# A gate polynomial refitted: one product moved from VectorE to a square on ScalarE, in an attention and feed-forward kernel on one core

## The chip, the cores and the metric

The kernel runs on one core of one Trainium2 chip. The metric is the device time of one execution in microseconds (us). TensorE is called PE, VectorE DVE, ScalarE ACT, GpSimd POOL and SyncE SP. The names in profile rows are those of the program's tiles without their buffer numbers; L165 is line 165 of the kernel before.

## What is computed

Causal attention by blocks of 64, over 8 batches of 8 heads with 576 positions and a head size of 64, and then a feed-forward layer with a gate of its own. All data are float32.

```python
def _attn_ref(q, k, v):                       # q, k, v: (8, 8, 576, 64)
    scores = np.matmul(q, k.transpose(0, 1, 3, 2)) / np.sqrt(64)
    scores = np.where(block_i >= block_j, scores, -1e9)   # blocks of 64 positions
    attn = np.exp(scores - np.max(scores, axis=-1, keepdims=True))
    attn = attn / (np.sum(attn, axis=-1, keepdims=True) + 1e-09)
    return np.matmul(attn, v)

def _moe_ref(x, w_in, w_out):                 # x: (4608, 512), w_in: (512, 2048)
    h = x @ w_in
    sp = np.maximum(h, 0.0) + np.log1p(np.exp(-np.abs(h)))
    g = h * erf(sp)
    return g @ w_out
```

The part that matters here is g = h * erf(softplus(h)). The factor erf(softplus(h)) is a smooth step, and the kernel computes it as a polynomial in tanh.

## The kernel before

The 64 heads are worked through one after the other (the loop at L650, one turn a head). For each head, POOL's queue and SP's queue load q and k (L383 to L385), POOL splits them into a high and a low part (L388, L389), PE computes scores for row maxima (L400), DVE reduces them (L403), PE computes the transposed scores (L446, L447), ACT takes the exponential (L451), and from the fourth batch on ACT and DVE split the probabilities into two float16 parts (L462, L463). PE multiplies with v (L495) and sums rows (L518). After each pair of heads the result is normalised (L577) and stored as a high and a low float16 part in a DRAM tile x_d (L579, L580).

The feed-forward layer runs in tiles of T = 256 tokens, 18 of them, and in units of two blocks of 128 hidden columns. There are 16 blocks, taken in two groups of 8 (g = 0 and 1), so each group has 4 units and the whole kernel 18 x 8 = 144 units. A unit is made by moe_unit: 24 matmuls up (L190: high and low parts of x with high and low parts of the weights) fill a PSUM tile h of 128 x 512, the gate makes from it a high part gh and a low part gl in float16, and 12 matmuls down (L199) add their products to a PSUM tile o. A unit's down steps are queued three units behind its up steps (LAG = 3). After the last unit of a group, store scales o into DRAM: for the first group through ACT (L242), for the second through DVE, which adds the first group's part (L240).

The gate works on one h tile of 128 x 512 in the buffers r0 (three of them) and r1 (two). ACT computes the tanh (L159; in two or more calls where a tile crosses two batches) and two squares (L160, L161), DVE three products that stay in SBUF (L162, L163, L164) and the final step, which reads h from PSUM (L165). Then ACT casts to float16 (L166) and POOL takes the remainder (L167). The h tile comes free with L165. There are two h tiles while attention runs (pool ps_h) and four after it (ps_h2).

What sets the order: the program lists attention and feed-forward steps in an interleaved order (merge, with 12 or 28 feed-forward steps a head, RATE), and the tile framework's scheduler then places every instruction into its engine's queue by its dependencies and its own estimates. Each engine takes its queue strictly in order, so a row that waits holds up every row behind it. After the last head the loop at L701 runs the remaining units alone.

Of the kernel before, what the change touches and what calls it, by code (L numbers as in the profile page):

```python
# [13 lines left out]
AF = mybir.ActivationFunctionType  # L14
ALU = mybir.AluOpType
# [2 lines left out]
PSUM = bass.MemoryType.PSUM  # L18

GS = 2.0**-16  # L20
PAR = (0.4999584099340646, -0.7997936477435295, [(-0.46191564159745396, 0.41170731705509067), (0.6792666015498814, 0.003215831458770746), (1.8262741166576089,), (-0.004337242892183685,), (-2.7410929714529355,)], 0.9999991931998524)


def f32(ap):
# [8 lines left out]
def tile_attention_moe(ctx: ExitStack, tc: tile.TileContext, qk, v, w, maskrows, sels, out):  # L33
    nc = tc.nc
# [39 lines left out]
    bias = {}  # L74

    def const(val):
        if val not in bias:
            t = cpool.tile([P, 1], F32, name=f"c{len(bias)}")
            nc.gpsimd.memset(t, val)
            bias[val] = t  # L80
        return bias[val]

    p0, p1, pars, fin = PAR
    (a1, b1), (a2, b2), (c3,), (c4,), (c5,) = pars
    R8, R4, R2 = GS**0.125, GS**0.25, GS**0.5
    a2, b2, c3, c5, fin = a2 * R8, b2 * R8, c3 * R4, c5 * R2, fin * GS
    eps = const(1e-9)
    for val in (p1, b1, b2):
        const(val)

    slots = [wpool.tile([P, 4, DM], F16, name=f"w{f}") for f in range(NF + 1)]
# [58 lines left out]
    def gate(h, name, t, g):  # L150

        nu = h.shape[1]
        n = nu * T
        flat = h.rearrange("p a b -> p (a b)")
        gh, gl = (mpool.tile([P, n], F16, tag=t_, name=f"{name}_{t_}", bufs=LAG + 1) for t_ in ("gh", "gl"))
        r0, r1 = (mpool.tile([P, n], F32, tag=t_, name=f"{name}_{t_}", bufs=k) for t_, k in (("r0", 3), ("r1", 2)))
        r0s = r0.rearrange("p (a b) -> p a b", b=T)
        for b, lo, hi in spans(t * T, T):
            nc.scalar.activation(r0s[:, :, lo:hi], h[:, :, lo:hi], AF.Tanh, bias=const(p1), scale=bss[b][g][:, 0:1])  # L159
        nc.scalar.activation(r1, r0, AF.Square, bias=const(b1), scale=a1)  # L160
        nc.scalar.activation(r0, r1, AF.Square, bias=const(b2), scale=a2)  # L161
        nc.vector.scalar_tensor_tensor(out=r0, in0=r0, scalar=c3, in1=r0, op0=ALU.add, op1=ALU.mult)  # L162
        nc.vector.scalar_tensor_tensor(out=r0, in0=r1, scalar=c4, in1=r0, op0=ALU.add, op1=ALU.mult)  # L163
        nc.vector.scalar_tensor_tensor(out=r0, in0=r0, scalar=c5, in1=r0, op0=ALU.add, op1=ALU.mult)  # L164
        nc.vector.scalar_tensor_tensor(out=r0, in0=r0, scalar=fin, in1=flat, op0=ALU.add, op1=ALU.mult)  # L165
        nc.scalar.copy(gh, r0)  # L166
        nc.gpsimd.tensor_tensor(out=gl, in0=r0, in1=gh, op=ALU.subtract)  # L167
        return gh, gl

    def spans(t0, n):  # L170

        for b in range(t0 // S, (t0 + n - 1) // S + 1):
            yield b, max(0, b * S - t0), min(n, (b + 1) * S - t0)
# [4 lines left out]
    def moe_unit(xh, xl, o, t, u, u0, u1, spread):  # L178

        turns.append(u)  # L180
        nu, name = 2, f"m{t}_{u}"
        h = hpools[len(turns) % len(hpools)].tile([P, nu, T], F32, tag="h", name=f"{name}_h")
        parts = []

        def up(k, cs):
            wf = wt[u * nu + k]
            for cc in cs:
                sl = slice(cc * P, (cc + 1) * P)
                for i, (a, x) in enumerate(((0, xh), (0, xl), (1, xh))):
                    nc.tensor.matmul(h[:, k, :], lhsT=wf[:, a, sl], rhs=x[:, cc, :], start=cc == 0 and i == 0, stop=cc == NCC - 1 and i == 2)  # L190
            if k == nu - 1 and cs[-1] == NCC - 1:
                parts.extend(gate(h, name, t, group[u * nu]))

        def down(k, c, lo):
            gh, gl = parts
            wf = wt[u * nu + k]
            sl = slice(k * T + c * P, k * T + (c + 1) * P)
            for a, b_ in (((gl, 2),) if lo else ((gh, 2), (gh, 3))):
                nc.tensor.matmul(o[c], lhsT=a[:, sl], rhs=wf[:, b_, :], start=u == u0 and k == 0 and not lo and b_ == 2,  # L199
                                 stop=u == u1 - 1 and k == nu - 1 and lo)  # L200

        edge = u in (u0, u1 - 1) or not spread
        return ([lambda k=k, cs=cs: up(k, cs) for k in range(nu) for cs in ((0, 1), (2, 3))],
                [lambda a=a: down(*a) for a in sorted(((k, c, lo) for k in range(nu) for c in range(T // P) for lo in (False, True)),
                                                      key=lambda a: (a[1], a[2], a[0]) if edge else (a[2], a[0], a[1]))])
# [534 lines left out]
```

## Time and profile before

| | |
|---|---|
| median of 3 runs | 1267.88 us (1267.43 to 1275.67) |
| profiled execution | 1269.5 us, its span 1267.5 us |
| granted TensorE clock, mean | 0.969 |
| mean of one tanh (L159), square (L160, L161) | 666, 720, 720 ns |
| mean of one product (L162, L163, L164), final step (L165) | 825, 840, 787, 679 ns |
| mean of one cast (L166), remainder (L167) | 617, 1220 ns |

The means are over the whole run. The span runs from the first to the last instruction, and the two microseconds beyond it lie around the program. A row of the profile's groups names line, engine, operation, output and inputs, and how often it ran; then its busy time and the mean of one in ns, and after the last bar the idle time of the engine just before these rows with what ended it. The chain of waits is followed back from the last instruction, at each step to what released it.

### The profile page before, as it was taken

To read this page: it belongs to the slowest core of one execution; us is meant where nothing else is said; L and a number is where in the kernel's file an instruction comes from. 1 tells how busy PE (TensorE), PEld (TensorE's weight loads), DVE (VectorE), ACT (ScalarE), POOL (GpSimd) and SP (SyncE) were. 2 spreads that over 40 slices of the span, in tenths; PEclk is the share of its full clock that TensorE was granted. 3 is DMA by queue.
4 is the path that set the end of the run, shared out by engine and by line. 5 is a ranking of instruction groups with operands and counts; after the bars stand their busy time and mean duration, and the time that the engine had idled before them with its cause. 6 is when DMAs were issued, how large, how long until landed. Compare 5 with 4: busy or idle time off the path is not lost.

```text
span 1267.5 us, 23446 instructions
## 1 busy us (share of the span) xinstructions
PE 1174.1 (93%) x9018; PEld 812.4 (64%) x9018; DVE 899.5 (71%) x1601; ACT 778.0 (61%) x1555; POOL 521.3 (41%) x485
## 2 busy tenths in 40 slices
PE   5698798989999999999999999999999999999996
PEld 3465465566666666667667676766667766666563
DVE  4587698888677777887768777778777755464554
ACT  2465575667565666666666666665766765555543
POOL 6355454536443343545434453535444313212211
PEclk9777799999999999999999999999999999999999
DMA  9987568654444455354444554454444221121111
GB/s 235 221 211 191 140 186 196 168 131 114 111 120 112 120 120 126 98 141 118 100 115 117 122 124 116 116 125 118 109 126 116 58 68 58 54 83 35 59 58 50
DMA packets 95740, 151.72 MB, mean 120 GB/s; under 512 B 7738, under 2 KB 44922, under 8 KB 95630
## 3 DMA queue, kind: packets, MB, share of 16 engines
q1 hardware_dynamic: 69840, 93.34, 25.3%
q0 software_dynamic: 25120, 56.66, 22.2%
q8 instruction: 71, 1.16, 0.4%
q10 hardware_dynamic: 670, 0.23, 0.1%
q14 instruction: 39, 0.32, 0.1%
HBM read 121.66 MB, written 28.31 MB: 118 GB/s over the span
## 4 chain that ended last, share of the span: by engine, by line
PE 37%; DVE 30%; ACT 17%; DMA 8%; issue 5%; POOL 2%; ACTq 0%; DVEq 0%; SPq 0%; POOLq 0%
PE m_h L190 12%; PE o L199 11%; DVE m_r L163 6%; DVE m_r L162 5%; DVE m_r L164 5%; DVE m_r L165 4%; ACT m_r L159 4%; ACT m_r L160 4%; ACT m_r L161 4%; PE u L495 4%; DMA qk<-qk 2%; PE t L446 2%; DVE mx L403 2%; PE s L400 2%; DMA qk<-mt 2%
## 5 line engine op out<-in xcount | busy, mean ns | idle before, releaser
L190 PE MATMUL m_h<-xh,w 128*128 128x256 f16 x2304 | 477.2, 276 | 25.6 <-DVE m_r L165 18.5
L190 PEld LDWEIGHTS <-w 128*128 128x128 f16 x3456 | 328.0, 99 | 164.2 <-issue 33.7
L167 POOL TENSOR_TENSOR m_gl<-m_r,m_gh 128x512 f16<-128x512 f32 x144 | 175.6, 1220 | 423.5 <-ACT m_gh L166 365.2
L199 PE MATMUL o<-w,m_gh 128*128 128x512 f16 x1152 | 335.4, 383 | 12.2 <-DVE pt L240 8.6
L190 PE MATMUL m_h<-xl,w 128*128 128x256 f16 x1152 | 317.1, 275 | 0.3 <-DMA xl<-x_d 0.3
L162 DVE SCALAR_TENSOR_TENSOR m_r<-m_r 128x512 f32<-128x512 f32 x144 | 118.8, 825 | 189.8 <-ACT m_r L161 172.8
L403 DVE TENSOR_REDUCE mx<-s 64x1 f32<-64x288 f32 (+4 forms) x384 | 174.4, 469 | 83.8 <-PE s L400 82.6
L451 ACT ACTIVATE p<-t 128x288 f32<-128x288 f32 (+4 forms) x384 | 144.8, 384 | 99.5 <-PE t L447 89.0
L166 ACT CAST m_gh<-m_r 128x512 f16<-128x512 f32 x144 | 88.8, 617 | 188.6 <-DVE m_r L165 188.1
L199 PE MATMUL o<-w,m_gl 128*128 128x512 f16 x576 | 203.6, 383 | 0.3 <-POOL m_gl L167 0.3
L446 PE MATMUL t<-qk 69*128 69x288 f32 (+4 forms) x384 | 168.4, 439 | 11.2 <-DMA qk<-mt 8.0
L400 PE MATMUL s<-qk 68*64 68x288 f32 (+3 forms) x384 | 151.3, 425 | 27.0 <-DMA qk<-qk 21.9
L159 ACT ACTIVATE m_r<-m_h,c,bs 128x512 f32<-128x512 f32 (+3 forms) x192 | 124.3, 666 | 57.4 <-PE m_h L190 55.1
L388 POOL TENSOR_TENSOR qk<-st,qk 64x576 fp32r<-64x576 f32 x64 | 96.9, 1514 | 116.7 <-DMA qk<-qk 113.9
L199 PEld LDWEIGHTS <-m_gh 128*128 128x128 f16 x1152 | 100.5, 99 | 68.0 <-issue 17.3
L163 DVE SCALAR_TENSOR_TENSOR m_r<-m_r,m_r 128x512 f32<-128x512 f32 x144 | 121.0, 840 | 2.8
L447 PE MATMUL t<-qk 128*128 128x288 f32 (+4 forms) x384 | 120.4, 314 | 0.0
L164 DVE SCALAR_TENSOR_TENSOR m_r<-m_r 128x512 f32<-128x512 f32 x144 | 113.3, 787 | 2.4
L389 POOL TENSOR_TENSOR qk<-st,qk 64x576 fp32r<-64x576 f32 x64 | 99.3, 1552 | 35.9 <-DMA qk<-qk 28.1
L463 DVE TENSOR_TENSOR p<-p,p 128x832 f16<-128x832 f32 x80 | 84.0, 1050 | 34.8 <-ACT p L462 34.8
L161 ACT ACTIVATE m_r<-m_r,c 128x512 f32<-128x512 f32 x144 | 103.7, 720 | 2.8 <-ACT m_r L160 1.0
L160 ACT ACTIVATE m_r<-m_r,c 128x512 f32<-128x512 f32 x144 | 103.7, 720 | 1.7
(99 smaller groups left out, 1457.9 us busy)
## 6 DMA issues: line engine op xcount, KB each, us to landing
qk<-qk POOLq DMA_DIRECT2D x64, 432.0 KB, 5.0
st<-qk SPq DMA_DIRECT2D x64, 288.0 KB
qk<-qk POOLq DMA_DIRECT2D x64, 288.0 KB, 5.3
raw<-w SPq DMA_DIRECT2D x32, 512.0 KB
v<-v SPq DMA_DIRECT2D x16, 640.0 KB
x_d<-xs POOLq DMA_DIRECT2D x32, 288.0 KB, 3.9
xh<-x_d SPq DMA_DIRECT2D x36, 256.0 KB
xl<-x_d SPq DMA_DIRECT2D x36, 256.0 KB
```

The source lines that it names most:

```text
L159: nc.scalar.activation(r0s[:, :, lo:hi], h[:, :, lo:hi], AF.Tanh, bias=const(p1), scale=bss[b][g][:, 0:1])
L160: nc.scalar.activation(r1, r0, AF.Square, bias=const(b1), scale=a1)
L161: nc.scalar.activation(r0, r1, AF.Square, bias=const(b2), scale=a2)
L162: nc.vector.scalar_tensor_tensor(out=r0, in0=r0, scalar=c3, in1=r0, op0=ALU.add, op1=ALU.mult)
L163: nc.vector.scalar_tensor_tensor(out=r0, in0=r1, scalar=c4, in1=r0, op0=ALU.add, op1=ALU.mult)
L164: nc.vector.scalar_tensor_tensor(out=r0, in0=r0, scalar=c5, in1=r0, op0=ALU.add, op1=ALU.mult)
L167: nc.gpsimd.tensor_tensor(out=gl, in0=r0, in1=gh, op=ALU.subtract)
L190: nc.tensor.matmul(h[:, k, :], lhsT=wf[:, a, sl], rhs=x[:, cc, :], start=cc == 0 and i == 0, stop=cc == NCC - 1 and i == 2)
L199: nc.tensor.matmul(o[c], lhsT=a[:, sl], rhs=wf[:, b_, :], start=u == u0 and k == 0 and not lo and b_ == 2, stop=u == u1 - 1 and k == nu - ...
L400: nc.tensor.matmul(dst[:r, :w_], lhsT=qh[:K, i * P : i * P + r], rhs=kh[:K, k0 : k0 + w_], start=True, stop=True)
L403: nc.vector.tensor_reduce(out=mx[:r, col : col + 1], in_=src, axis=AX.X, op=ALU.max, negate=True)
L446: nc.tensor.matmul(s[:kk, :w_], lhsT=kh[:K, ks], rhs=qh[:K, q0 : q0 + w_], start=True, stop=False)
```

## The change

The step function is fitted anew, with another arrangement of the same kind of operations. With t the tanh, u the first square and v the second, the polynomial before was, up to constants, y = (v + c3) v, z = (u + c4) y, w = (z + c5) z, and the result (w + fin) h. Now a third square s of an affine function of v replaces y, z = (s + c4) u, and the rest stays: three squares on ACT, two products and the final step on DVE.

```diff
-PAR = (0.4999584099340646, -0.7997936477435295, [(-0.46191564159745396, 0.41170731705509067), (0.6792666015498814, 0.003215831458770746), (1.8262741166576089,), (-0.004337242892183685,), (-2.7410929714529355,)], 0.9999991931998524)
+PAR = (0.49996096731559087, -0.7971597824113146, [(-0.3568271365965769, 0.32141033078193654), (-0.6157408373309642, -4.092496034124806e-06), (4.2811914462809915, 1.199366796860444), (-1.4383868560728355,), (-2.741088145004764,)], 1.0000005263157887)
...
-    (a1, b1), (a2, b2), (c3,), (c4,), (c5,) = pars
-    R8, R4, R2 = GS**0.125, GS**0.25, GS**0.5
-    a2, b2, c3, c5, fin = a2 * R8, b2 * R8, c3 * R4, c5 * R2, fin * GS
+    (a1, b1), (a2, b2), (a3, b3), (c4,), (c5,) = pars
+    R4, R2 = GS**0.25, GS**0.5
+    a3, b3, c4, c5, fin = a3 * R4, b3 * R4, c4 * R2, c5 * R2, fin * GS
     eps = const(1e-9)
-    for val in (p1, b1, b2):
+    for val in (p1, b1, b2, b3):
         const(val)
...
         nc.scalar.activation(r1, r0, AF.Square, bias=const(b1), scale=a1)
         nc.scalar.activation(r0, r1, AF.Square, bias=const(b2), scale=a2)
-        nc.vector.scalar_tensor_tensor(out=r0, in0=r0, scalar=c3, in1=r0, op0=ALU.add, op1=ALU.mult)
-        nc.vector.scalar_tensor_tensor(out=r0, in0=r1, scalar=c4, in1=r0, op0=ALU.add, op1=ALU.mult)
+        nc.scalar.activation(r0, r0, AF.Square, bias=const(b3), scale=a3)
+        nc.vector.scalar_tensor_tensor(out=r0, in0=r0, scalar=c4, in1=r1, op0=ALU.add, op1=ALU.mult)
         nc.vector.scalar_tensor_tensor(out=r0, in0=r0, scalar=c5, in1=r0, op0=ALU.add, op1=ALU.mult)
         nc.vector.scalar_tensor_tensor(out=r0, in0=r0, scalar=fin, in1=flat, op0=ALU.add, op1=ALU.mult)
```

The line numbers stay: L162 is a product on DVE before and the third square on ACT after, L163 and L164 are the two products, L165 the final step. The constant b3 is one more tile, set by POOL at the start.

Since the scheduler goes by the operations it finds, the rows around the gate change places as well. Below is ACT's queue around the gate of one unit (tile m_5, while head 26 gives way to head 27), before. Rows of p are exponentials and casts of the attention, mt belongs to the row maxima, m_6 to the next gate.

```order
L159 ACTIVATE m_5_r_4378<-m_5_h,c_83,bs_1_113 128x2x192
L451 ACTIVATE p_1_140<-t_26_256_4399 128x320
L160 ACTIVATE m_5_r_4379<-m_5_r_4378,c_85 128x512
L462 CAST p_26_4138<-p_1_140 128x768
L161 ACTIVATE m_5_r_4378<-m_5_r_4379,c_87 128x512
L451 ACTIVATE p_0_139<-t_27_0_4422 128x288
L451 ACTIVATE p_0_139<-t_27_288_4448 128x288
L432 CAST mt_4460<-mt_4458 5x128
L433 DMA qk_126<-mt_4460 1x5x128
L159 ACTIVATE m_6_r_4473<-m_6_h,c_83,bs_1_111 128x2x64
L166 CAST m_5_gh<-m_5_r_4378 128x512
```

The same place of ACT's queue after the change.

```order
L159 ACTIVATE m_5_r_4380<-m_5_h,c_83,bs_1_115 128x2x192
L451 ACTIVATE p_1_142<-t_26_256_4401 128x320
L160 ACTIVATE m_5_r_4381<-m_5_r_4380,c_85 128x512
L462 CAST p_26_4140<-p_1_142 128x768
L161 ACTIVATE m_5_r_4380<-m_5_r_4381,c_87 128x512
L451 ACTIVATE p_0_141<-t_27_0_4424 128x288
L162 ACTIVATE m_5_r_4380<-m_5_r_4380,c_89 128x512
L451 ACTIVATE p_0_141<-t_27_288_4450 128x288
L432 CAST mt_4462<-mt_4460 5x128
L433 DMA qk_128<-mt_4462 1x5x128
L159 ACTIVATE m_6_r_4475<-m_6_h,c_83,bs_1_113 128x2x64
L166 CAST m_5_gh<-m_5_r_4380 128x512
```

One exponential that stood behind the last square now stands ahead of it. DVE's queue for the same gate, before; mx are the attention's row maxima, pt an accumulated output tile.

```order
L463 TENSOR_TENSOR p_26_4138<-p_1_140,p_26_4138 128x768
L162 SCALAR_TENSOR_TENSOR m_5_r_4378<-m_5_r_4378 128x512
L403 TENSOR_REDUCE mx_145<-s_29_4432 128x1
L163 SCALAR_TENSOR_TENSOR m_5_r_4378<-m_5_r_4379,m_5_r_4378 128x512
L403 TENSOR_REDUCE mx_145<-s_29_4432 128x1
L164 SCALAR_TENSOR_TENSOR m_5_r_4378<-m_5_r_4378 128x512
L240 SCALAR_TENSOR_TENSOR pt_0_4395<-o_1_0_3729,bs_1_111,pt_0_4395 128x512
L165 SCALAR_TENSOR_TENSOR m_5_r_4378<-m_5_r_4378,m_5_h 128x512
```

And after.

```order
L463 TENSOR_TENSOR p_26_4140<-p_1_142,p_26_4140 128x768
L403 TENSOR_REDUCE mx_147<-s_29_4434 128x1 x2
L163 SCALAR_TENSOR_TENSOR m_5_r_4380<-m_5_r_4380,m_5_r_4381 128x512
L240 SCALAR_TENSOR_TENSOR pt_0_4397<-o_1_0_3731,bs_1_113,pt_0_4397 128x512
L164 SCALAR_TENSOR_TENSOR m_5_r_4380<-m_5_r_4380 128x512
L403 TENSOR_REDUCE mx_147<-s_29_4456 128x1
L165 SCALAR_TENSOR_TENSOR m_5_r_4380<-m_5_r_4380,m_5_h 128x512
```

Two reductions left the gate for the place ahead of its first product, and one came in. In the last units, where no attention is left, ACT's queue before reads as follows.

```order
L159 ACTIVATE m_1_r_14536<-m_1_h,c_83,bs_0_124 128x512
L160 ACTIVATE m_1_r_14537<-m_1_r_14536,c_85 128x512
L161 ACTIVATE m_1_r_14536<-m_1_r_14537,c_87 128x512
L159 ACTIVATE m_2_r_14593<-m_2_h,c_83,bs_0_124 128x512
L160 ACTIVATE m_2_r_14594<-m_2_r_14593,c_85 128x512
L166 CAST m_1_gh<-m_1_r_14536 128x512
L161 ACTIVATE m_2_r_14593<-m_2_r_14594,c_87 128x512
```

After the change the same two gates stand so.

```order
L159 ACTIVATE m_1_r_14538<-m_1_h,c_83,bs_0_126 128x512
L160 ACTIVATE m_1_r_14539<-m_1_r_14538,c_85 128x512
L161 ACTIVATE m_1_r_14538<-m_1_r_14539,c_87 128x512
L162 ACTIVATE m_1_r_14538<-m_1_r_14538,c_89 128x512
L159 ACTIVATE m_2_r_14595<-m_2_h,c_83,bs_0_126 128x512
L166 CAST m_1_gh<-m_1_r_14538 128x512
L160 ACTIVATE m_2_r_14596<-m_2_r_14595,c_85 128x512
```

The next gate's first square (L160 of m_2) stood ahead of the cast of m_1 and now stands behind it.

## The prediction

> **What bounds the kernel now.** I read the page's busy times first, then three stretches, then the chain of waits of each stretch, then the instructions of each stretch. The first 150 us hold attention and weight conversion and only the start of the first gate, so they are left aside. The page, the table by stretch, and that of L165 alone for one stretch: 13 gates end in 150 to 300 us, 88 in 300 to 1000 us (rows below), and so 43 of the 144 after that.
>
> ```profile
> PE 1174.1 (93%) x9018; PEld 812.4 (64%) x9018; DVE 899.5 (71%) x1601; ACT 778.0 (61%) x1555; POOL 521.3 (41%) x485
> ...
> core 0: us, PE busy (x) PEld busy (x) DVE busy (x) ACT busy (x) POOL busy (x), PEclk, DMA share, GB/s
> 150.00:300.00 150.00, 135.98 (x1004) 91.16 (x1003) 130.95 (x244) 100.58 (x231) 72.11 (x61) 0.97 0.62 158
> 300.00:1000.00 700.00, 679.27 (x5586) 482.80 (x5585) 529.42 (x935) 459.45 (x903) 313.17 (x284) 1.00 0.48 117
> 1000.00:1267.00 267.00, 248.68 (x1779) 166.47 (x1776) 143.61 (x210) 145.83 (x243) 58.40 (x52) 0.99 0.18 58
> ...
> 150.00:300.00 150.00, 8.71 (x13) 0.97 0.62 158
> ```
>
> PE looks like the bound: 679.3 of 700 us. But a busy PE of this profile is not PE at its peak, so the chain decides. Its shares by line for the same three stretches, in order:
>
> ```profile
> by line: PE o L199 7.6%; DMA raw<-w 7.5%; DVE w L123 7.2%; DVE w L122 7.0%; DVE m_r L163 6.0%; DVE mx L403 5.9%; DVE m_r L164 5.2%; DVE w L147 5.1%; PE m_h L190 4.9%; PE us L518 4.3%; DVE m_r L162 3.8%; DVE m_r L165 3.7%; PE s L400 3.2%; PE
> ...
> by line: PE m_h L190 16.1%; PE o L199 15.3%; DVE m_r L163 5.7%; DVE m_r L162 5.6%; issue 5.0%; DVE m_r L164 4.9%; ACT m_r L159 3.9%; DVE m_r L165 3.4%; PE u L495 3.2%; ACT m_r L160 3.0%; ACT m_r L161 2.9%; DVE p L463 2.8%; DVE mx L403 2.6%;
> ...
> by line: PE m_h L190 9.4%; PE o L199 9.3%; DVE m_r L162 8.8%; DVE m_r L163 8.8%; ACT m_r L161 8.8%; DVE m_r L165 8.5%; ACT m_r L160 8.1%; DVE m_r L164 7.6%; issue 7.5%; ACT m_r L159 6.5%; ACT m_gh L166 4.7%; DVE pt L240 2.2%; PE u L495 1.5%
> ```
>
> The gate stands beside PE on the chain everywhere. In 300 to 1000 us its DVE rows hold 5.7 + 5.6 + 4.9 + 3.4 = 19.6% and its ACT rows 3.9 + 3.0 + 2.9 = 9.8%: 29.4%, or 206 us. In the tail they hold, with the cast L166, 61.8%. The gate's own work in 300 to 1000 us, first DVE, then ACT (columns: busy, mean ns of one, idle before):
>
> ```profile
> L403 DVE TENSOR_REDUCE mx<-s 64x1 f32<-64x288 f32 (+2 forms) x238 | 108.7, 468 | 37.6 <-PE s L400 37.1
> L163 DVE SCALAR_TENSOR_TENSOR m_r<-m_r,m_r 128x512 f32<-128x512 f32 x88 | 78.4, 891 | 1.4
> L463 DVE TENSOR_TENSOR p<-p,p 128x832 f16<-128x832 f32 x74 | 77.8, 1051 | 28.3 <-ACT p L462 28.3
> L162 DVE SCALAR_TENSOR_TENSOR m_r<-m_r 128x512 f32<-128x512 f32 x88 | 77.1, 876 | 81.6 <-ACT m_r L161 66.6 <-ACT p L451 6.6 <-ACT mt L432 3.8
> L164 DVE SCALAR_TENSOR_TENSOR m_r<-m_r 128x512 f32<-128x512 f32 x88 | 72.3, 822 | 1.1
> L165 DVE SCALAR_TENSOR_TENSOR m_r<-m_r,m_h 128x512 f32<-128x512 f32 x88 | 59.6, 677 | 1.2
> ...
> L240 DVE SCALAR_TENSOR_TENSOR pt<-o,bs,pt 128x512 f32<-128x512 f32 (+1 forms) x24 | 17.8, 740 | 0.3 <-PE o L199 0.3
> ...
> L451 ACT ACTIVATE p<-t 64x64 f32<-64x64 f32 (+2 forms) x238 | 91.2, 385 | 67.6 <-PE t L447 62.0 <-PE s L400 1.6 <-DMA qk<-mt 1.2
> L159 ACT ACTIVATE m_r<-m_h,c,bs 128x512 f32<-128x512 f32 (+3 forms) x117 | 75.4, 665 | 22.0 <-PE m_h L190 20.2 <-PE t L447 0.8 <-PE vt L338 0.8
> L462 ACT CAST p<-p 128x832 f16<-128x832 f32 x74 | 63.3, 856 | 1.4
> L161 ACT ACTIVATE m_r<-m_r,c 128x512 f32<-128x512 f32 x87 | 62.7, 721 | 1.6 <-ACT m_r L160 0.8
> L160 ACT ACTIVATE m_r<-m_r,c 128x512 f32<-128x512 f32 x87 | 62.7, 721 | 0.8
> L166 ACT CAST m_gh<-m_r 128x512 f16<-128x512 f32 x88 | 54.3, 617 | 106.0 <-DVE m_r L165 105.8
> ```
>
> The reader should see a loop. ACT runs a gate's tanh and squares, DVE its products, ACT then waits for L165 (105.8 us here) and casts in L166; the next gate's squares mostly stand behind that cast in ACT's order. One round of it is 75.4/88 = 0.86 (tanh) + 2 x 0.72 + 0.62 on ACT and 0.876 + 0.891 + 0.822 + 0.677 = 3.27 on DVE: 6.2 us of a period of 700/88 = 7.95 us, the rest being attention work in between. Without the cast it is 5.57 us x 88 = 490 us. The chain holds 206 of these, so about 42% of a gate's change is paid by the clock; the rest of the time PE sets the pace. PE too meets the gate's end, through the two PSUM tiles of h:
>
> ```profile
> PE m_h L190 <- DVE m_r L165: 12.3, 13, 1.9
> ```
>
> **The change, part by part.** *One product less on DVE.* Its first three products vary far more than the last (ns min/median/max over the whole run):
>
> ```profile
> L162 DVE SCALAR_TENSOR_TENSOR m_r<-m_r x144: 628/693/2168, 149.5 to 1255.1; 128x512 f32<-128x512 f32 x144
> L163 DVE SCALAR_TENSOR_TENSOR m_r<-m_r,m_r x144: 670/691/2721, 150.7 to 1255.8; 128x512 f32<-128x512 f32 x144
> L164 DVE SCALAR_TENSOR_TENSOR m_r<-m_r x144: 622/691/1899, 151.4 to 1256.5; 128x512 f32<-128x512 f32 x144
> L165 DVE SCALAR_TENSOR_TENSOR m_r<-m_r,m_h x144: 620/681/690, 152.4 to 1257.3; 128x512 f32<-128x512 f32 x144
> ```
>
> The median is 0.69 us, the mean in 300 to 1000 us is (876 + 891 + 822)/3 = 863 ns. L165, whose second input is the PSUM tile, never exceeds 690 ns, so the excess is something that meets inputs in SBUF, and POOL is busy 313 us there. The product's price lies between 0.691 (all the excess moves to the two products left) and 0.863 us (it leaves with its share). I take 0.863, since the excess is spread evenly over three like instructions.
>
> *One square more on ACT.* It has the form of L161: 0.721 us, and the nearest rows leave no other value. It needs no new table:
>
> ```profile
> L432 ACT ACT_TABLE_LOAD x1 | 1.3, 1283 | 7.0 <-issue 7.0
> ...
> L79 POOL MEMSET c<- 128x1 f32 x4 | 0.2, 98 | 0.3 <-POOLq L733 0.3
> ```
>
> The square's bias is a fifth memset on POOL, ahead of the first loads of qk: +0.1 us. SP's few rows that change places are loads and stores issued early; I cost them at nothing, the cover being the double buffers of st, x and pt, and at a few us between both signs if that cover is gone.
>
> *The rows that change sides.* The scheduler packs attention work into the gate differently. I counted rows in the two orders over the 93 gates that follow the first 14, up to the last 37. Between a gate's tanh and its last square ACT has 102 exponentials (L451) instead of 73 and 24 casts (L462) instead of 9: (29 x 0.385 + 15 x 0.856)/93 = +0.26 us a gate. Between the first and the last product DVE has 48 reductions (L403) instead of 75 and 23 subtractions (L463) instead of 42, and 4 fewer of the accumulations at 0.74 us (L240): (27 x 0.468 + 19 x 1.051 + 4 x 0.74)/93 = -0.38 us. These DVE rows now stand between the last product of one gate and the first of the next, where DVE waits for ACT anyway (66.6 us before L162 above); that wait is their cover.
>
> *The loop in 300 to 1000 us:* +0.72 + 0.26 on ACT, -0.863 - 0.38 on DVE: -0.26 us a gate. Paid at 42%: 88 x 0.26 x 0.42 = -9.7 us.
>
> *150 to 300 us:* the chain holds 18.7% of 150 us in DVE products, 28 of 13 x 3.27 = 42.5 us, or 66%. 13 x 0.26 x 0.66 = -2.2 us. DVE is at 131 of 150 us here, so its relief is worth at least that.
>
> *The tail.* DVE and then ACT between 1060 and 1250 us:
>
> ```profile
> L162 DVE SCALAR_TENSOR_TENSOR m_r<-m_r 128x512 f32<-128x512 f32 x34 | 26.2, 771 | 84.4 <-ACT m_r L161 82.4 <-POOL m_gl L167 2.0
> L164 DVE SCALAR_TENSOR_TENSOR m_r<-m_r 128x512 f32<-128x512 f32 x33 | 22.8, 691 | 1.1
> ...
> L159 ACT ACTIVATE m_r<-m_h,c,bs 128x512 f32<-128x512 f32 (+3 forms) x45 | 29.2, 659 | 17.8 <-PE m_h L190 17.7
> L161 ACT ACTIVATE m_r<-m_r,c 128x512 f32<-128x512 f32 x34 | 24.5, 721 | 0.9
> L166 ACT CAST m_gh<-m_r 128x512 f16<-128x512 f32 x33 | 20.4, 617 | 64.7 <-DVE m_r L165 64.7
> ```
>
> Here POOL does little and a product is 0.691, so the trade costs +0.03 us a gate. A round is 0.77 + 3 x 0.69 on DVE and 29.2/33 + 2 x 0.72 + 0.62 on ACT, 5.8 us, and 43 of them 249 us, of which the chain holds 61.8% of 267 = 165: 66% is paid, 43 x 0.03 x 0.66 = +0.9 us. Before, the next gate's first square stood ahead of this gate's cast in 4 of the last 36 pairs, now in none; its tanh in 21, now 22. That loses 4 x 0.72 and gains one tanh of 0.66, at 66%: +1.5 us. What is late next there is the same loop, not PE.
>
> Sum: -9.7 - 2.2 + 0.9 + 1.5 + 0.1 = -9.4 us. The profiled execution took 1269.5 us (span 1267.5), 1.6 above the median of 1267.88: 1260.1 against its own time, 1258.5 against the median. I say 1260.
>
> **The rivals.**
>
> *A, the loop pays in full.* If PE's place on the chain is only slack that the gate leaves, 88 x 0.26 = -23 us, -3.4 and a tail of +3.5 at full price: about -23, so 1246. For it: a round of 7.95 us nearly equals the gate's 6.2 plus the work packed in between. Against it: PE is busy 679 of 700 us and leads the chain with L190 and L199.
>
> *B, the product saves only its undisturbed time.* POOL's instructions are as many as before; if they meet the two products that are left as often as the three, the loop changes by 0.98 - 0.691 - 0.38 = -0.09: -3.3, -0.8 and +2.5, together -1.6, so about 1267. For it: the maxima of 2 to 2.7 us look like a wait for a whole POOL instruction. Against it: with fewer such products there are fewer meetings. The Trainium skill, "SBUF — State Buffer", section "Who interferes with whom", says that a VectorE instruction with two SBUF inputs and a GpSimd instruction that reads SBUF lock each other out for a whole instruction, and that one SBUF input is free of it; L165's maximum of 690 ns against 2721 agrees. The Trainium skill, "ScalarE: Activation LUTs", section "Rules for kernel authors", speaks against the change: it gives multiplies to VectorE as the faster engine. The tail agrees by 0.03 us (691 against 721 ns), the middle stage disagrees (863 against 721); by that rule the sum would be this rival's.
>
> *C, ACT's longer queue is paid and DVE's emptier one is not.* The DVE rows moved out of the gate would delay the next gate's first product, and the product saves 0.691: +0.98 - 0.69 = +0.29 us a gate. At the same shares +10.7, +2.5 and +2.5: about 1285. It decides from +0.22 us a gate on, where the loss passes 1%. For it: exponentials that wait for PE (62.0 us before L451) now stand ahead of 29 more last squares. Against it: DVE's 66.6 us of waiting before the first product, as cover.
>
> **How the numbers follow.** A measurement of this kernel tells about 1%, or 12.7 us, from no change: below 1255.2 is faster, above 1280.6 slower. Forecast 0.47 (its own range 1252 to 1267), A 0.25, B 0.16, C 0.12. Faster is A and the low end of the forecast, 0.25 + 0.07 = 0.32; the same is the rest of the forecast and B, 0.40 + 0.16 = 0.56; slower is C, 0.12. The range from 1244 to 1276 holds A's and B's times and leaves out C and the worst of A.
>
> **What would show it.** DVE's busy time should fall by about 144 x 0.83 = 119 us to 780, ACT's rise by 104 to 882, which makes ACT the busier of the two. If the product left with its excess, the two SBUF products left keep means near 0.86 in the middle stage; near 0.95 they have taken it over (B). ACT's wait for L165 in that stage should shrink well below 105.8 us, and the gate's share of the chain there from 29% to some 27%. PE's wait for L165 should not grow. The forecast is wrong if the tail from 1000 us on gets longer by more than 5 us, if waits before L451 or at PE for exponentials grow (C), or if the middle stage ends more than 15 us earlier (A).

## The result, and the profile after

The changed kernel takes 1253.1 us (median of 4 runs, 1248.7 to 1255.0) where the kernel before took 1268.0 on the same chip: a ratio of 0.9854, interval 0.982 to 0.9889. The two medians by themselves stand at 0.988, inside that interval. In a second session it took 1244.9 against 1272.1, ratio 0.9808 (0.9768 to 0.9848). By the two ratios it is faster by 1.5 and 1.9%. The time lies inside the predicted range, 7 and 15 us below the predicted 1260 in the two sessions, and on the other side of the 1% mark from the case that the prediction held likeliest.

The page's busy times of the changed kernel, and then its table by stretch (columns as in the prediction: PE, PEld, DVE, ACT, POOL busy with their counts, granted clock, DMA share, GB/s).

```profile
PE 1169.7 (93%) x9018; PEld 811.0 (65%) x9018; DVE 791.9 (63%) x1457; ACT 865.4 (69%) x1699; POOL 515.9 (41%) x486
```

```profile
150.00:300.00 150.00, 140.10 (x1042) 95.44 (x1043) 126.10 (x240) 113.71 (x255) 76.77 (x65) 0.98 0.63 163
300.00:1000.00 700.00, 685.88 (x5645) 488.38 (x5644) 468.95 (x857) 517.15 (x1003) 308.92 (x284) 1.00 0.48 117
1000.00:1252.00 252.00, 232.62 (x1680) 155.25 (x1678) 102.36 (x148) 162.60 (x262) 54.15 (x48) 0.99 0.19 59
```

ACT is now the busier of the two, as the change has it. In 150 to 300 us PE does 1042 matmuls where it did 1004, and in 300 to 1000 us 5645 where it did 5586. So the time was gained in both stretches.

A table by fixed times shows this badly, since each stage ends at another time. The next table goes by gates instead: the start of the final step (L165) of the first gate, and the time from one such start to another. Gate 0 to 20 is the stage in which weights are still being converted, 20 to 106 the long middle, 106 to 143 about the tail. The numbers are worked out from the start times of the final steps in each trace; the other kernels of the table come below. The profiled execution of the one with the new gate in the middle only was a slow one (1270.7 us, the median of its nine runs 1259.9), so its numbers up to gate 20 are in brackets and are not used.

```
us              gate 0 starts  0-4   4-13  13-20   4-20   20-106  106-143
before              152.4     37.8  112.7   54.9  167.5   686.5   213.1
changed             152.6     38.6  104.2   57.4  161.6   677.1   211.9
changed, again      146.9     38.3  104.2   57.2  161.4   674.3   212.6
early only          145.2     38.0  105.6   56.2  161.8   685.8   213.2
middle only        (159.3)   (38.1)(118.1) (56.1)(174.3)  673.8   213.3
tail only           153.9     37.9  114.9   55.1  170.0   685.5   212.6
work alone          149.4     39.2  116.9   54.9  171.9   676.0   209.0
order alone         157.1     39.8  117.1   57.1  174.2   702.6   211.6
PE's order undone   144.8     41.0  114.5   57.9  172.4   675.3   212.1
product left out    146.8     38.5  114.2   56.2  170.3   667.9   205.9
square added        154.5     37.6  119.9   58.1  177.9   713.3   210.3
cast on DVE         148.7     38.5  116.6   58.7  175.3   663.4   199.1
cast on DVE late    152.4     39.9  104.7   57.7  162.4   666.3   199.2
```

Between the two profiled executions that is +0.2 (start) + 0.8 - 8.5 + 2.5 - 9.4 - 1.2 = -15.6 us, and their spans differ by 15.5. The forecast had -2.2 for the early stage, -9.7 for the middle and +2.4 for the tail. The middle came out as forecast; the early stage and the tail did not.

The gate's rows of the changed kernel in 300 to 1000 us (busy, mean ns, idle before and what ended it). L162 is now the third square.

```profile
L451 ACT ACTIVATE p<-t 128x320 f32<-128x320 f32 (+2 forms) x241 | 92.2, 384 | 51.1 <-PE t L447 46.2 <-PE s L400 1.6 <-PE vt L338 0.8
L164 DVE SCALAR_TENSOR_TENSOR m_r<-m_r 128x512 f32<-128x512 f32 x89 | 81.9, 920 | 1.8
...
L163 DVE SCALAR_TENSOR_TENSOR m_r<-m_r,m_r 128x512 f32<-128x512 f32 x89 | 74.7, 840 | 73.7 <-ACT m_r L162 67.2 <-ACT p L451 5.8
...
L162 ACT ACTIVATE m_r<-m_r,c 128x512 f32<-128x512 f32 x89 | 64.1, 720 | 1.1 <-ACT m_r L161 0.3
...
L166 ACT CAST m_gh<-m_r 128x512 f16<-128x512 f32 x88 | 54.3, 617 | 85.3 <-DVE m_r L165 83.3 <-DMA qk<-mt 1.8
```

The square costs 0.720 us, as forecast. The products took 876 + 891 + 822 ns and now take 840 + 920: 0.829 us less where 0.863 was forecast. ACT's wait for L165 fell from 105.8 to 83.3 us, and the wait ahead of the exponentials (L451) from 67.6 to 51.1. Durations over the whole run, as min/median/max:

```profile
L163 DVE SCALAR_TENSOR_TENSOR m_r<-m_r,m_r x144: 627/692/1901, 150.6 to 1240.3; 128x512 f32<-128x512 f32 x144
L164 DVE SCALAR_TENSOR_TENSOR m_r<-m_r x144: 668/691/1916, 151.5 to 1241.0; 128x512 f32<-128x512 f32 x144
L165 DVE SCALAR_TENSOR_TENSOR m_r<-m_r,m_h x144: 621/686/689, 152.6 to 1241.8; 128x512 f32<-128x512 f32 x144
```

The two products left are still the ones that are sometimes stretched, and the step with one input in PSUM never is. That is again as the Trainium skill, "SBUF — State Buffer", section "Who interferes with whom", has it for POOL and two SBUF inputs on VectorE.

The chain by line in 300 to 1000 us, first in the changed kernel's profile here, then in that of its second session.

```profile
by line: PE m_h L190 21.8%; PE o L199 21.2%; PE u L495 4.6%; DVE m_r L164 4.3%; DVE m_r L163 4.2%; PE s L400 3.3%; PE t L446 3.2%; PE t L447 3.0%; issue 3.0%; ACT m_r L159 2.7%; DVE m_r L165 2.6%; ACT m_r L160 2.2%; ACT m_r L161 2.2%; ACT m
```

```profile
by line: PE m_h L190 18.0%; PE o L199 17.4%; DVE m_r L163 5.3%; DVE m_r L164 5.1%; PE u L495 4.0%; issue 3.9%; DVE m_r L165 3.6%; ACT m_r L159 3.2%; ACT m_r L161 2.9%; ACT m_r L160 2.8%; ACT m_r L162 2.7%; PE s L400 2.7%; PE t L446 2.7%; PE
```

The gate held 29.4% of this stretch. Now it holds 18.2% here, with L162's row cut off at the end (at most 2.2 more, since the rows are sorted), and 25.6% there. The same program gives two shares that are at least 5 points apart, so the share shows a direction and is a poor multiplier. PE waits less for the gate (the third number is the longest wait):

```profile
PE m_h L190 <- DVE m_r L165: 8.3, 11, 2.1
```

DVE and ACT between 1050 and 1240 us, in the tail:

```profile
L163 DVE SCALAR_TENSOR_TENSOR m_r<-m_r,m_r 128x512 f32<-128x512 f32 x33 | 22.9, 694 | 101.8 <-ACT m_r L162 101.7
L164 DVE SCALAR_TENSOR_TENSOR m_r<-m_r 128x512 f32<-128x512 f32 x33 | 22.8, 691 | 1.1
...
L166 ACT CAST m_gh<-m_r 128x512 f16<-128x512 f32 x34 | 21.0, 618 | 55.1 <-DVE m_r L165 55.1
```

The products take 694 + 691 where three took 771 + 691 + 691 or a little less: here too the product that went was the one with some excess.

### The profile page after: what moved, and what is told of

It is laid out like the page before. It is cut to its first block, busy times and chain, and to the rows that moved or that the text cites. A ratio compares the mean times of both kernels' runs of the same rounds, so it can differ in the third digit from the quotient of the medians.

```text
span 1252.0 us, 23446 instructions
## 1 busy us (share of the span) xinstructions
PE 1169.7 (93%) x9018; PEld 811.0 (65%) x9018; DVE 791.9 (63%) x1457; ACT 865.4 (69%) x1699; POOL 515.9 (41%) x486
## 4 chain that ended last, share of the span: by engine, by line
PE 49%; DVE 20%; ACT 18%; DMA 7%; issue 4%; POOL 1%; DVEq 0%; SPq 0%; POOLq 0%; ACTq 0%
PE m_h L190 16%; PE o L199 15%; PE u L495 5%; DVE m_r L163 4%; DVE m_r L164 4%; DVE m_r L165 3%; ACT m_r L160 3%; ACT m_r L162 3%; ACT m_r L161 3%; ACT m_r L159 3%; PE t L446 3%; PE s L400 3%; PE t L447 2%; DMA qk<-qk 2%; DMA qk<-mt 2%
## 5 line engine op out<-in xcount | busy, mean ns | idle before, releaser
L190 PE MATMUL m_h<-xh,w 128*128 128x256 f16 x2304 | 476.1, 276 | 19.5 <-DVE m_r L165 12.2
L199 PE MATMUL o<-w,m_gh 128*128 128x512 f16 x1152 | 334.1, 382 | 12.2 <-DVE pt L240 4.9
L167 POOL TENSOR_TENSOR m_gl<-m_r,m_gh 128x512 f16<-128x512 f32 x144 | 171.8, 1193 | 391.1 <-ACT m_gh L166 340.6
L163 DVE SCALAR_TENSOR_TENSOR m_r<-m_r,m_r 128x512 f32<-128x512 f32 x144 | 112.8, 783 | 197.3 <-ACT m_r L162 190.8
L451 ACT ACTIVATE p<-t 128x288 f32<-128x288 f32 (+4 forms) x384 | 144.6, 384 | 79.4 <-PE t L447 69.1
L199 PEld LDWEIGHTS <-m_gh 128*128 128x128 f16 x1152 | 100.2, 98 | 67.6 <-issue 12.3
L164 DVE SCALAR_TENSOR_TENSOR m_r<-m_r 128x512 f32<-128x512 f32 x144 | 122.6, 852 | 3.3
L161 ACT ACTIVATE m_r<-m_r,c 128x512 f32<-128x512 f32 x144 | 103.8, 721 | 2.7 <-ACT m_r L160 0.7
L162 ACT ACTIVATE m_r<-m_r,c 128x512 f32<-128x512 f32 x144 | 103.7, 720 | 2.3 <-ACT m_r L161 0.3
L160 ACT ACTIVATE m_r<-m_r,c 128x512 f32<-128x512 f32 x144 | 103.7, 720 | 1.6
```

Source lines behind the costliest of these rows:

```text
L163: nc.vector.scalar_tensor_tensor(out=r0, in0=r0, scalar=c4, in1=r1, op0=ALU.add, op1=ALU.mult)
L451: nc.scalar.activation(p32s[part][:kk, c : c + w_ - skip], s[:kk, skip:w_], AF.Exp, scale=SCALE)
```

## Experiments

**Where does the gain come from: three kernels with the new gate in one stage each.** Both polynomials stand in the program, and the gate's number n chooses: the line below is that of the early kernel, the middle one has 14 < n <= 107 and that of the tail n > 107. All else is the scheduler's.

```diff
+        gates.append(name)
+        n = len(gates)
+        new = n <= 14
...
+        if new:
+            nc.scalar.activation(r1, r0, AF.Square, bias=const(b1), scale=a1)
...
+        else:
+            nc.scalar.activation(r1, r0, AF.Square, bias=const(e1), scale=d1)
...
```

Expected of the early one:

> The new gate in the first 14 units only, the old one in the 130 others; both give the reference's step function. By theory 1 (VectorE is the bound while weights are converted, so a product less per gate is paid several times over there, as the 8.5 us between the fourth and eighth gate of the changed kernel suggest) the time falls by 4 to 9 us against the kernel before, nearly all of it won before 300 us. By theory 2 (the same loop everywhere, -0.11 us a gate; the early jump is chance of that one order) it falls by less than 2.5 us.

of the middle one:

> The new gate in units 15 to 107 only. By theory 1 the loop of ScalarE and VectorE pays 0.10 us a gate with attention around it: 7 to 11 us less than the kernel before, growing evenly from 310 to 1040 us. By theory 2 with all of the gain in the loop: 12 to 15 us less. If the products' relief is worth nothing outside the early stage: within 3 us of the kernel before.

and of the tail:

> The new gate in the last 37 units only. By the working of the prediction (a square is 0.03 us longer than an undisturbed product, and four squares lose their place ahead of a cast) 1 to 3 us more than the kernel before; by the trace of the changed kernel, in which the last 37 units take as long as before within 0.5 us, no difference: within 1 us.

Measured, as ratios to the kernel before: early 0.9925 (0.9898 to 0.9951), middle 0.9903 (0.9859 to 0.9946), tail 0.9981 (0.995 to 1.0012). In us of 1270.7 these are -9.5, -12.3 and -2.4, together 1.9%. That is the whole change (1.5 and 1.9% in its two sessions) within the intervals, so the stages add up. In the table above, the early and the middle kernel gain in the stage that has the new gate, 161.8 us early and 673.8 in the middle; their other stages, those in brackets aside, stay within 1 us of before. The early stage, with 14 of 144 gates, brings nearly as much as the middle with 93. The tail shows no gain that this measurement can tell from nothing. Against what was expected, the early kernel gained a little more than 4 to 9 us, the middle one lies between its first two cases, and in the tail the 1 to 3 us more did not come. (The 8.5 us in the first expectation are those between gates 4 and 13; between gates 4 and 8 the two traces differ by 74.8 - 65.3 = 9.5 us.)

**Work without order: the changed kernel's instructions in the order of before.** A changed kernel moves hundreds of rows besides the ones that it edits. Here every engine's queue is pinned by issue-order dependencies between neighbours, to the order of before; the third square stands right behind the second.

```diff
+def pin(tc):
...
+    ins = {i.name: i for i in tc.nc.cur_bb.bb.instructions}
+    info = mybir.DependencyInfo(mybir.DependencyClass.NoSync, mybir.DependencyReason.DATA)
...
+            if prev is not None:
+                tc.add_manual_dep(cur, prev.name, info, reason="order")
+            prev = cur
```

> The instructions of the changed kernel, held on every engine to the order of the kernel before, the third square right behind the second. By the prediction's sum without its moved rows the loop changes by 0.72 - 0.86 = -0.14 us a gate, at 42% in the middle -5 us, and the early stage pays once more what its VectorE is relieved of: 5 to 12 us less than the kernel before under theory 1. Theory 2: within 3 us of it.

It takes 1256.8 us, ratio 0.9881 (0.9852 to 0.991): 15 us less, more than the 5 to 12 expected. Its gate rows in 300 to 1000 us; the lines are shifted by 98, so L261 and L262 are the products, L260 the third square, L264 the cast.

```profile
L261 DVE SCALAR_TENSOR_TENSOR m_r<-m_r,m_r 128x512 f32<-128x512 f32 x89 | 76.7, 861 | 88.3 <-ACT m_r L260 78.2 <-ACT p L549 9.1 <-POOL qk L486 0.8
L262 DVE SCALAR_TENSOR_TENSOR m_r<-m_r 128x512 f32<-128x512 f32 x89 | 73.1, 821 | 1.1
...
L264 ACT CAST m_gh<-m_r 128x512 f16<-128x512 f32 x89 | 54.8, 616 | 73.6 <-DVE m_r L263 73.5
```

The product saves 876 + 891 + 822 - 861 - 821 = 907 ns here, more than its own mean. The middle is 676.0 us, as short as with the new order (677.1 and 674.3). So in the middle the trade alone makes the gain, and beside the new gate the moved rows add nothing that these runs can show. The early stage, 171.9 us, shows no gain. The tail is 209.0, 3 us shorter than with the new order.

**Order without work: the kernel before, in the changed kernel's order.** The reverse: before's instructions pinned to the changed kernel's queues, the third product right ahead of its gate's next product. The edit is the same function with another list.

> The instructions of the kernel before, held on every engine to the order of the changed kernel, each removed product right ahead of its gate's next product. Theory 1 (the gain is the work that left VectorE): the new order without the lighter gate is worth little, within 4 us of the kernel before. Theory 2 (the gain, and the early part above all, is the scheduler's new order): 8 to 15 us less than the kernel before.

It takes 1295.8 us, ratio 1.0156 (1.0108 to 1.0203): slower, which neither case expected. Its cast in 300 to 1000 us (L264 again):

```profile
L264 ACT CAST m_gh<-m_r 128x512 f16<-128x512 f32 x85 | 52.5, 618 | 132.6 <-DVE m_r L263 132.5
```

ACT waits 132.5 us for the final step where it waited 105.8, and fewer gates fit into the stretch (85). An order that was made for a gate of two products delays a gate of three: the middle takes 702.6 us. Its early stage (gate 4 to 13 in 117.1 us) gains nothing either.

**Is it TensorE's order that makes the early gain?** In these traces neither the work nor the order brings it alone. The next kernel is the changed kernel with only TensorE's queue pinned to its order of before; ACT and DVE keep nearly the changed kernel's order (by their traces).

> The changed kernel with TensorE alone held to its order of before; the scheduler places the other engines around it. Theory 3 (lighter gates win the early 6 to 9 us only with the order that TensorE has in the changed kernel, where the up matmuls of a unit come earlier): 168 us or more between the fourth and the twentieth gate, and about 1257 to 1262 us on this chip's scale of 1272 before. Theory 4 (ScalarE's and VectorE's new order do it): 160 to 164 us there, and the changed kernel's time within 4 us.

It takes 1260.0 us, ratio 0.9911 (0.9877 to 0.9945). The middle keeps its gain (675.3) and the early stage loses it: 114.5 us from gate 4 to 13, and 172.4 to gate 20. The stretch from 150 to 300 us of this kernel, and then that of the one with the work alone:

```profile
150.00:300.00 150.00, 136.86 (x977) 91.11 (x975) 111.56 (x215) 104.27 (x234) 67.18 (x59) 0.93 0.62 153
```

```profile
150.00:300.00 150.00, 133.30 (x979) 89.80 (x980) 115.69 (x224) 104.42 (x235) 67.89 (x61) 0.94 0.63 156
```

DVE is relieved in both, 112 and 116 us busy where it had 131, and nothing is gained by it: PE gets 977 and 979 matmuls done, the changed kernel 1042. Counted from gate 4 to 13, DVE is busy for 82 and 87 us in these two, 88 us in the changed kernel and 97 us before, so the relief is there with and without the gain. The new gate with TensorE's new order is found in the changed kernel, in the one with the new gate early, and in the last one of the table (cast on DVE late): by their traces the matmuls come in the same order up to the 2490th, at some 400 us, past this stage. In their four executions gates 4 to 13 take 104.2 to 105.6 us; all others take 112.7 to 119.9. The kernel with the order alone has the changed kernel's order of matmuls throughout, but the old gate, and is among the others. The orders of before and after part at the 690th matmul, among the first gate's down steps. One of the places that differ is shown here, from TensorE's queue. Before:

```
LDWEIGHTS w
MATMUL m_1_h<-xh_1,w 128x256
MATMUL t_13_128<-qk 128x448 x2
LDWEIGHTS m_2_gh
MATMUL o_0_1<-w,m_2_gh 128x512
LDWEIGHTS m_2_gh
MATMUL o_0_1<-w,m_2_gh 128x512
LDWEIGHTS m_2_gh
MATMUL o_0_0<-w,m_2_gh 128x512
MATMUL s_15_1<-qk 64x288
```

And after the change:

```
LDWEIGHTS w
MATMUL m_1_h<-xl_1,w 128x256
MATMUL s_15_1<-qk 64x288
LDWEIGHTS w
MATMUL m_1_h<-xh_1,w 128x256
LDWEIGHTS m_2_gh
MATMUL o_0_1<-w,m_2_gh 128x512
LDWEIGHTS m_2_gh
MATMUL o_0_1<-w,m_2_gh 128x512
MATMUL t_13_256<-qk 128x320 x2
```

The attention's scores (s_15 and the next piece of t_13) come earlier among the up steps (m_1_h) and the down steps (m_2_gh). That these rows and no others of the new order make the gain was not tried.

The traces show two more things that go along with the gain. All of it lies between gates 4 and 8, which take 65.1 to 66.4 us in the four executions and 74.8 to 79.9 us in all others. There PE was busy for 66.0 us and idle for 8.7 before, and busy for 60.3 and idle for 5.0 after. The granted clock, read from gate 4 to 7 and from 7 to 8, is 0.96 or 1.00 in the four; in every other kernel one of the two parts has 0.86 to 0.93. And in four of the others (the work alone, the product left out, the square added, the cast on DVE) PE waits there once, for 4.3 to 6.2 us, for a part of x to be loaded for an up step. This is that wait in the kernel with the work alone:

```profile
PE m_h L288 <- DMA xl<-x_d: 4.8, 1, 4.8
```

In the four it does not occur. Whether the new order gains by itself, or by keeping such waits and the lower clock away, stays open.

**The two halves by themselves.** First the kernel before without its first product (L162) and with nothing in its place; that product is left out of the step function.

```diff
-        nc.vector.scalar_tensor_tensor(out=r0, in0=r0, scalar=c3, in1=r0, op0=ALU.add, op1=ALU.mult)
```

> The kernel before without its first product (L162), and no square in its place: the product is left out of the computation. If the price of a product on the path is what theory 1 says (0.86 us and the rows it holds up, at some 42%), the time falls by 144 x 0.86 x 0.42 = 52 us at most and, as TensorE takes over, rather by 25 to 40. If TensorE covers the gate mostly, by less than 20.

It takes 1241.3 us, ratio 0.9763 (0.9721 to 0.9805). Then the kernel before with one more square on ACT behind the second, which changes the step function.

```diff
+        nc.scalar.activation(r0, r0, AF.Square, bias=const(b2), scale=a2)
```

> The kernel before with one more square on ScalarE behind the second (so that the step function is another one) and all products kept. If the trade is the sum of its two halves, the product's 30 us less (measured alone) and the whole change's 18 to 27 less leave 3 to 12 us more for the square. If ScalarE's queue is what is paid at 0.72 us a gate and 42% or more: 25 us more or above.

It takes 1298.5 us, ratio 1.021 (1.0165 to 1.0255). So a product less is worth -30 us, as expected, and a square more +27 where the sum of halves asked for 3 to 12: large, nearly equal, and each at its own schedule. A part of the 27 may be the clock's: the six runs with the square were granted 0.956 to 0.966 on the mean, the kernel before 0.964 to 0.972 beside them. Their sum is -3 us where the change measures -15 to -27. Two halves timed apart say little about a trade whose parts are this near to each other.

**The loop: take the cast off ACT.** If the loop of the prediction (ACT, then DVE, then ACT's cast, with the next squares behind it) sets part of the pace, then the cast on DVE, right behind L165, shortens it.

```diff
-        nc.scalar.copy(gh, r0)
+        nc.vector.tensor_copy(gh, r0)
```

> The changed kernel with the cast L166 on VectorE in place of ScalarE. If the loop is what theory 1 says (ScalarE stands still for L165 until it has cast, and the next squares stand behind the cast), taking the cast off ScalarE lets the next gate's squares run beside this gate's products: 20 us or more below the changed kernel, half of it after 1000 us. If TensorE or the PSUM tiles of h set the pace, within 5 us of the changed kernel.

It takes 1241.7 us, ratio 0.9757 (0.9723 to 0.979). In all that is only 3 us below the changed kernel of the same session, and the two intervals overlap; 20 or more was expected. The stages tell why. The middle falls by 11 us against the changed kernel's second session, to 663.4, and the tail by 13.5, to 199.1. The early stage gives 14 back (175.3). TensorE's order is another one there, a cast more stands on DVE, and PE waits 6.2 us for a load of x; which of these takes the early gain away was not separated.

**Both gains.** The cast on ACT for the first 14 units and on DVE from the 15th on.

```diff
+        gates.append(name)
...
-        nc.scalar.copy(gh, r0)
+        (nc.scalar.copy if len(gates) <= 14 else nc.vector.tensor_copy)(gh, r0)
```

> The changed kernel with the cast L166 on VectorE from the 15th unit on and on ScalarE before it. The trace of the kernel with every cast on VectorE is 11 us shorter than the changed one from the 20th to the 106th gate and 12 us shorter after it, but loses 14 before the 20th. If these add, 20 to 24 us below the changed kernel, 40 to 50 below the kernel before. If the early loss belongs to the order and stays, 6 to 12 below the changed kernel.

It takes 1227.7 us, ratio 0.9655 (0.9622 to 0.9688): 3.4% below the kernel before, 44 us, and 0.9655/0.9808 = 0.984 of the changed kernel by their ratios, some 20 us. So the parts add as the first case had it. Its early stage is 162.4 us, its middle 666.3, its tail 199.2. The chain of its middle stage (300 to 1000 us; lines shifted by 4):

```profile
by line: PE m_h L194 28.8%; PE o L203 28.1%; PE u L499 6.3%; PE s L404 4.3%; PE t L450 4.2%; PE t L451 4.0%; PE us L522 2.4%; issue 2.0%; PE rt L560 1.8%; DVE m_r L168 1.8%; DVE m_r L167 1.8%; PE rb L579 1.6%; DVE p L467 1.4%; DMA v<-v 1.2%
```

The gate has nearly left it: PE's two large rows hold 56.9%, and no gate row is above 1.8%. The DVE cast itself, in the middle stage and then between 1050 and 1220 us:

```profile
L170 DVE CAST m_gh<-m_r 128x512 f16<-128x512 f32 x90 | 51.3, 571 | 1.2
```

```profile
L170 DVE CAST m_gh<-m_r 128x512 f16<-128x512 f32 x32 | 13.6, 425 | 1.0
```

It takes less than ACT's 617 ns in both, and since it stands right behind L165 on the same queue it waits for 1.2 and 1.0 us in all, where ACT's cast waited for 85.3 and 55.1.

**The changed kernel once more**, on the chip of the experiments on order.

> The changed kernel unchanged, beside the two runs above on the same chip: 11 to 21 us less than the kernel before under every theory. Its second trace tells what of the early stage's 6 us between the fourth and the twentieth gate comes again: all of it under theory 1, between none and 12 if it is chance of one execution.

1244.9 us, ratio 0.9808 (0.9768 to 0.9848), as told above. Its interval just overlaps that of the first session.

## Why the prediction was right, and where it was not

*The loop, right.* That ACT, DVE and ACT's cast share a loop which sets part of the pace beside PE is what the cast on DVE shows: 11 us in the middle and 13 in the tail from one instruction that changes engine, and 8 and 13 in the kernel with the late cast. The move ends ACT's wait and makes ACT's queue lighter by a cast at the same time; these two were not tried apart.

*The middle, -9.7 forecast, -9.4 and -12.2 measured: right in sum, wrong in its parts.* The forecast made 5.3 us of it from the trade (0.143 x 88 x 42%) and 4.4 from the moved rows. The kernel with the work alone gains 10.5 us without any moved row (676.0), and the changed kernel's two executions stand 1.1 us above it and 1.7 below. The kernels with the new gate in the middle only and with PE's order undone have yet other orders and lie at 673.8 and 675.3. So the moved rows paid about nothing that shows above the 3 us between two executions. The trade paid more: by the work kernel's own rows it is 0.907 - 0.721 = 0.186 us a gate, 16 us for 86 gates, and 10.5 of 16 is 66%, not 42%. The two errors cancelled; that the middle's sum came out is luck. The failed step is "Paid at 42%", a share of the chain taken as a price; the chain's own share moved from at most 20.4 to 25.6% between two executions of one program.

*The product's price, right.* 0.863 forecast, 0.829 and 0.907 measured. Rival B's 0.691 is out, though not all of the excess left: L164 went from 822 to 920 ns in the new order.

*150 to 300 us, -2.2 forecast, about -6 measured: wrong.* The profiled pair gives 167.5 - 161.6 = 5.9 us; the early kernel by itself is 9.5 us faster (6 to 13). The failed step is "DVE is at 131 of 150 us here, so its relief is worth at least that". With DVE relieved to 112 and 116 us the stage was no shorter. The gain shows only where the lighter gate and TensorE's new order stand together, beside a higher granted clock and fewer waits of PE; the prediction did not look at TensorE's queue there at all, and the cause stays open.

*The tail, +2.4 forecast, -1.2 and -0.5 measured: wrong in size.* The trade was set at +0.03 us a gate with the product at 0.691, although the row quoted for L162 said 771 ns. By the rows it is 0.721 - (771 + 691 + 691 - 694 - 691)/1000 = -0.05 us, or -1.7 us for 37 gates. The work alone gained 4.1 us there; the other 2.4 are not settled. The kernel with a square added has a tail of 210.3 us where the kernel before has 213.1, so another order alone can move the tail by 3 us. The lost overlap was forecast at +1.5 us; the new order's tail is 211.9 and 212.6 against 209.0, so the order as a whole costs +2.9 to +3.6. The sign was right; that the lost overlap is what costs it is not shown.

*The busy times.* DVE was forecast at 780 and has 791.9, ACT at 882 and has 865.4. The terms were right as sums over groups (a square is 0.720 us; the groups' busy times add up to 972 us before and 852 after on DVE, and to 861 and 964 on ACT), but an engine's busy time is less than that sum, since the records of neighbours overlap. The timeline of ACT in the changed kernel, as start and duration:

```profile
601.68 0.62 ACT L166 CAST m_gh<-m_r 128x512 f16<-128x512 f32 x1 [0.45 <-DVE m_r L165]
602.21 0.40 ACT L451 ACTIVATE p<-t 128x288 f32<-128x288 f32 x1
602.51 0.77 ACT L159 ACTIVATE m_r<-m_h,c,bs 128x512 f32<-128x512 f32 x1
603.32 0.72 ACT L160 ACTIVATE m_r<-m_r,c 128x512 f32<-128x512 f32 x1
604.07 0.72 ACT L161 ACTIVATE m_r<-m_r,c 128x512 f32<-128x512 f32 x1
```

The cast ends at 602.30 by its record and the next row starts at 602.21. Rows that need the one before, as the squares do, don't overlap: 603.32 to 604.07 is 0.75 us.

*The rivals.* A (the loop pays in full) would have had the middle 23 us shorter and the tail 3.5 longer; both are refuted, though its 1246 lies near the second session's time. C (ACT's longer queue) needed longer waits ahead of L451, and they shrank from 67.6 to 51.1 us. It was not idle, though: the new order with the old work comes near to what C feared, and it costs 1.6%, by the wait for L165 and not by that ahead of the exponentials (69.6 us).

*The chances.* "The same" had 0.56 and "faster" 0.32, and both intervals lie beyond 1%. The early stage's missing 4 to 7 us and the tail's 3 make that difference.

## What to carry to other kernels

When an edit changes an instruction's engine, the scheduler's new order is a second change, and it can be worth as much as the first or be harmful by itself; compare every engine's queue, that of the bottleneck too, before the edit is priced. A chain's share shows which loop matters but is no price: take the price from a run that shortens that loop by a known time. Where an in-order queue ends a loop with a small step that waits for another engine, as the cast here, try to put that step on the engine that it waits for, and check each stage of the kernel: here it gained from the 15th unit on and not over the whole.

## What was not expected of the hardware

The start varies by itself. TensorE's queue is the same up to the first gate's down steps in the kernel before, the changed kernel and the one with the late cast on DVE, and yet the first gate's final step starts up to 5.7 us apart, and that in two executions of one program, the changed kernel. The granted clock (the third number from the end) differs there between executions. The stretch from 100 to 150 us of the kernel before, of the changed kernel's second session, and of the kernel with the late cast:

```profile
100.00:150.00 50.00, 39.45 (x255) 27.31 (x255) 32.28 (x77) 28.21 (x65) 23.89 (x20) 0.73 0.69 158
```

```profile
100.00:150.00 50.00, 42.77 (x285) 30.32 (x286) 41.20 (x92) 32.94 (x75) 22.77 (x22) 0.79 0.72 158
```

```profile
100.00:150.00 50.00, 45.20 (x264) 30.47 (x264) 39.77 (x83) 31.46 (x71) 24.37 (x22) 0.66 0.77 179
```

0.73, 0.79 and 0.66 go with starts at 152.4, 146.9 and 152.4 us, so a low clock goes with a late start, though not in proportion. In all 13 traces of the table the clock of this stretch is 0.74 or more where the first gate starts by 149.4 us and 0.73 or less where it starts at 152.4 or later; which brings the other is not shown. The middle stage looks steadier: with the old gate it lasted 685.5 to 686.5 us in the three kernels that have it there in the scheduler's own order (before, early only, tail only), one execution each, while single runs of the kernel before lie between 1260 and 1277 us. How a measured gain is spread over the stages is therefore read from gate to gate and not from the start of the span.

The product and the cast on DVE have no fixed price either: 0.69 us for a product in the tail and 0.82 to 0.92 in the middle, 0.425 us for a cast in the tail and 0.571 in the middle, where POOL is busy for 309 of 700 us in the changed kernel. A square on ACT takes 0.720 us in both.
